# Passes of bias group 7 behind six rows of the last group, and later routing steps of the first sequence issued one by one

## The chip, the core and the metric

One core of a Trainium2 chip runs the whole kernel. Its engines run side by side, each in the order in which its instructions were issued: PE multiplies matrices, DVE and ACT work on rows, POOL issues most of the transfers, SP the others. They wait for each other by semaphores. The metric is the device time of the core in microseconds.

## The reference

Eight sequences of 576 positions go through attention with 8 heads of 64. The scores get a bias that a small network of 32 hidden units makes of the two positions alone. The result, 4608 tokens of 512, then goes through one of eight experts, named by the token's domain.

```python
scores = scale * np.matmul(q, k.transpose(0, 1, 3, 2))
x = (psi_rel / psi_i)[..., None]        # log1p(|i - j|) / log1p(max(i, 1))
bias = np.maximum(x @ w1 + b1, 0.0) @ w2
attn = softmax(scores + bias.transpose(2, 0, 1)[None])
x = (attn @ v).transpose(0, 2, 1, 3).reshape(4608, 512)
for e in range(8):
    mask = domain_id == e
    out[mask] = np.maximum(x[mask] @ w1[e], 0.0) @ w2[e]
```

## The kernel before

**Bias stage.** The bias depends on no input of a sequence, so it is made once. Nine groups (ib 0 to 8) of 64 query positions each take 16 rows: tiles hr of 128 x 576, four positions times 32 hidden units, made by DVE (L203) or ACT (L200). PE multiplies the rows with the output weights in three passes (L222, L227): key chunks 0 and 1, chunks 2 and 3, and the last 64 keys. Each pass fills one tile of a ring of three PSUM tiles (named sc). ACT takes the exponential of each pass (L237, L233, for the last group L244) into the bias tables biasM, biasR, biasL and biasRL. Of chunk 3 DVE also copies the raw bias of two heads (L241, into biasW), out of the tile of the second pass. The rows of group ib + 1 are issued ahead of the passes of group ib.

In between stand steps of other work: the routing steps (below), a memset of pad words (L254) with a DMA on SP that fills the buffer x_dram (L255, named fire_x, 9.25 MB), and the first transposes of q and k on PE, with the copies out of PSUM that at.take issues (L500, L509).

**Attention.** A round of units follows for each sequence. A unit (scores) is a pair of heads and a key chunk: m00 to m33 (head pair, chunk), r0 and r1 for the last 64 keys, l0, l1 and x for the last 64 queries. Each takes a tile of the same ring; PE writes scores into it, ACT takes the exponential (L562, named e) and DVE multiplies by the bias (L573), often two units at once. PE then multiplies by v (L586, L590, accumulator pu), and DVE divides by the sums (L616, L617). The order of units and other steps is written out by hand in ROUND. In the first sequence the last group's passes come behind units m03, m10 and m11, and the transposes of head pairs 2 and 3 behind unit m01.

**Routing.** A generator (_phase_route) yields after each of its small steps on DVE, which make of the domains the place posi of each token in x_dram. Each next(route) issues one step. Finished rows of a sequence are scattered by posi (L647).

**Experts.** x_dram is read back transposed (L792, tile xT) and each expert's two layers run on PE (L803, L779), with weights loaded by POOL (L741).

Of the kernel before, what the change touches and what calls it, by code (L numbers as in the profile page):

```python
# [68 lines left out]
def rap(t, off, dims, nparts=None):  # L69
    p0 = list(t.ap[0])  # L70
    if nparts is not None:
        p0[1] = nparts
    return bass.AP(tensor=t.tensor, offset=off, ap=[p0] + [list(d) for d in dims])
# [111 lines left out]
def _phase_bias(tc, G, route, at, x_dram):  # L185


    nc = tc.nc
    fsb = G.bias_pools.enter_context(tc.tile_pool(name="fsb", bufs=1, side="right"))
    def hidden(ib, between=None):  # L190
        hrl = []
        for k16 in range(16):
            if ib < 8:
                r, a = ib // 2, 16 * (ib % 2) + k16
                m, c0 = 32 * r + a, C4 - (16 * a + r)
            else:
                m, c0 = 128 + k16, W4 + C1 - 4 * k16
            hr = fsb.tile([P, S], F16, tag="hr", name="hr", bufs=34)
            if k16 in ((2, 5, 8, 11, 14) if ib < 2 else (3, 8, 13)):
                nc.scalar.activation(out=hr, in_=G.L4[:, c0: c0 + S], func=AF.Relu,  # L200
                                     bias=G.pb1[:], scale=G.slope[:, m: m + 1])
            else:
                nc.vector.tensor_scalar(out=hr, in0=G.L4[:, c0: c0 + S],  # L203
                                        scalar1=G.slope[:, m: m + 1], scalar2=G.nb1[:],
                                        op0=AO.mult, op1=AO.max)
            hrl.append(hr)
            if (ib, k16) == (0, 7):
                G.slopes(16, NGR)
            if (ib, k16) in ((1, 1), (1, 5), (1, 9), (2, 1), (2, 5)):
                next(route)  # L210
            if between is not None and k16 == between[0]:
                at.take(0, between[1])
        return hrl

    def outputs(ib, hrl):
        for jcs in ((0, 1), (2, 3), (4,)):
            eb = G.ring()
            for k16 in range(16):
                for lj, jc in enumerate(jcs):
                    hr = hrl[k16]  # L220
                    if jc < 4:
                        nc.tensor.matmul(out=eb[:, lj, 32 * k16: 32 * k16 + 32],  # L222
                                         lhsT=rap(hr, jc, [[4, 128]]),
                                         rhs=G.W2BIG[:, 0:32], start=True, stop=True)
                    else:
                        for h2 in range(2):
                            nc.tensor.matmul(out=eb[64 * h2: 64 * h2 + 64, 0, 16 * k16: 16 * k16 + 16],  # L227
                                             lhsT=hr[:, 512:576],
                                             rhs=rap(G.W2BIG, h2, [[2, 16]]), start=True, stop=True)
            ebv = eb.rearrange("p l (i h) -> p l h i", h=8)  # L230
            i0 = 64 * ib
            if jcs[0] == 4:
                nc.scalar.activation(out=G.biasR[:, :, i0: i0 + 64] if ib < 8 else G.biasRL,  # L233
                                     in_=eb[:, 0, 0:256].rearrange("p (i q) -> p q i", q=4),
                                     func=AF.Exp, bias=0.0, scale=0.125)
            elif ib < 8:
                nc.scalar.activation(out=G.biasM[:, jcs[0]: jcs[0] + 2, :, i0: i0 + 64], in_=ebv,  # L237
                                     func=AF.Exp, bias=0.0, scale=0.125)
                for lj, jc in enumerate(jcs):
                    if jc in RAW:  # L240
                        nc.vector.tensor_copy(out=G.biasW[jc][:, :, i0: i0 + 64], in_=ebv[:, lj, RAW[jc]:, :])  # L241
            else:
                for lj in range(2):
                    nc.scalar.activation(  # L244
                        out=G.biasL[:, jcs[0] // 2, lj, :, :, :].rearrange("p h q i -> p q h i"),
                        in_=ebv[:, lj, :, :].rearrange("p (q h) i -> p q h i", h=2),
                        func=AF.Exp, bias=0.0, scale=0.125)
            yield

    hrl = hidden(0)  # L250
    for ib in range(9):
        after = hidden(ib + 1, {6: (3, (4,)), 7: (1, (0, 1))}.get(ib)) if ib < 8 else None
        if ib == 1:
            nc.vector.memset(G.zero.rearrange("p o (r d) -> p (o r) d", r=4)[:, :, DM:].bitcast(I32), PAD)  # L254
            nc.sync.dma_start(out=x_dram.rearrange("(p c r) d -> p c (r d)", p=P, r=4),  # L255
                              in_=G.zero.to_broadcast([P, NSLOT // P // 4, 4 * XW]))
        for _ in outputs(ib, hrl):
            if ib == 8:
                yield
        if ib == 0:  # L260
            next(route)
        if ib in (5, 6):
            at.transposes(0, (4,) if ib == 5 else (0, 1), G.acc())
        if ib == 7:
            yield
        hrl = after


def _load_domains(tc, G, moe_domain_id):
# [140 lines left out]
class _Attention:  # L410
# [250 lines left out]
    def run(self, bias, route, late):  # L661
        G = self.G
        units = [("r", 0)] + [("m", p, c) for p in (0, 1) for c in range(4)] + [("r", 1)] + \
                [("m", 2, c) for c in range(4)] + [("l", 0), ("l", 1), ("x",)] + \
                [("m", 3, c) for c in range(4)]
        self.joined = {("l", 0): 0, ("l", 1): 1}
        for p in range(4):
            n = 4 if all(2 * p < RAW.get(c, H) for c in range(4)) else 2
            self.joined.update({("m", p, c): c % 2 for c in range(n)})
        names = {"".join(map(str, u)): ui for ui, u in enumerate(units)}  # L670
        jobs = {}

        def unit(b, name):
            if b >= B:
                return
            ui = names[name]
            jobs[b, name] = self.scores(b, units[ui])
            if b == 0 and name in LAST_ROWS:
                for _ in range(LAST_ROWS[name]):
                    next(bias, None)  # L680
            if (b, name) == (0, "m01"):
                self.transposes(0, (2, 3), G.acc())
                self.take(0, (2, 3))
            if b == 0 and ui > 2:
                for _ in range(2):
                    next(route, None)
            if b < B - 2 and ui == 3:
                self.load_qk(b + 2)
            if b < B - 2 and ui == 5:
                self.load_v(b + 2)  # L690
                self.load_last(b + 2)
            if b < B - 2 and ui == 7:
                self.load_vrag(b + 2)
            late(b, ui)

        def act(what, b):
            if what[0] in "TD":
                ps = tuple(map(int, what[1:]))
                if b + 1 < B:
                    if what[0] == "T":  # L700
                        self.transposes(b + 1, ps, self.G.ring())
                    else:
                        self.take(b + 1, ps)
            elif b < 0 or b >= B:
                pass
            elif what == "V":
                self.make_vext(b)
            elif what[0] == "W":
                self.weight(jobs.pop((b, what[1:])))
            elif what[0] == "A":  # L710
                p, c = int(what[1]), int(what[2])
                if c == 0:
                    self.av_begin(b, p)
                self.av(b, p, c)
                if (b, p) == (B - 1, 3) and c % 2 == 1:
                    self.norm(b, p, (c // 2,))
            elif what[0] == "N" and (b, int(what[1])) != (B - 1, 3):
                self.norm(b, int(what[1]))

        next(bias)  # L720
        unit(0, "r0")
        for b in range(B + 1):
            for what in ROUND:
                if what.rstrip("+") in names:
                    unit(b + what.count("+"), what.rstrip("+"))
                else:
                    act(what.rstrip("'"), b - what.count("'"))
# [162 lines left out]
def kernel(  # L890
# [24 lines left out]
    with tc.manual_schedule(engines={ET.PE, ET.DVE, ET.Activation}):  # L915
        with ExitStack() as att:
# [20 lines left out]
            at = _Attention(tc, G, q, k, v, x_dram)  # L937
            at.start()
            bias = _phase_bias(tc, G, route, at, x_dram)
            def late(b, ui):  # L940
                if (b, ui) == (0, 7):
# [47 lines left out]
```

## Time and profile before

| | us |
|---|---|
| median of three timed runs | 380.25 |
| lowest, highest | 378.14, 381.24 |
| profiled execution | 375.47 |
| its span, first to last instruction | 373.5 |
| busy: PE, DVE, ACT, POOL | 318.8, 234.9, 247.8, 181.4 |

The rows further down are from the profiled execution, with times from the start of its span. Its own time is 375.47 us, of which 373.5 are span. Bias rows and passes run until about 50 us, attention until about 216 us, the experts after that.

### The profile page before, as it was taken

Reading aid. Unit: us, or ns where it says so; the run is one execution under the profiler, and the core shown is the slowest. Engines: PE = TensorE matmul, PEld = TensorE weight load, DVE = VectorE, ACT = ScalarE, POOL = GpSimd, SP = SyncE. Lnnn points to the kernel's source line nnn. Section 1 sums busy time; section 2 is a strip of 40 time slices with the busy share of each in tenths; the row PEclk is TensorE's granted clock in tenths of the full one; section 3 lists DMA queues with packets and bytes.
Section 4 is the critical chain, followed back from the end, with each engine's and each line's share of the span. In section 5 each row is a group of like instructions: output and inputs, shape, how many; then the busy total and the mean of one; then the engine's idle time right before and its main releaser. Section 6 shows DMA issues by size and latency. Waiting matters only on the chain. (4 is left out here: it accounts for less than half of the span.)

```text
span 373.5 us, 9583 instructions
## 1 busy us (share of the span) xinstructions
PE 318.8 (85%) x4082; PEld 210.8 (56%) x4082; DVE 234.9 (63%) x436; ACT 247.8 (66%) x297; POOL 181.4 (49%) x220
## 2 busy tenths in 40 slices
PE   1499978689888888989897779999999699999892
PEld 0387946556565655656565545656463365565550
DVE  6999979899999999999999951221202002222121
ACT  8999969799999989999999933324150142332320
POOL 9360006318786888879664253525254027232322
PEclk9999999899999999999999999999999699999998
DMA  5999999989999999999998517999999999420212
GB/s 85 180 133 330 371 379 155 147 139 151 158 208 153 145 152 189 156 143 159 141 201 151 100 50 145 137 207 208 212 182 214 185 169 232 134 100 37 100 43 85
DMA packets 90995, 61.30 MB, mean 164 GB/s; under 512 B 43461, under 2 KB 85189, under 8 KB 90952
## 3 DMA queue, kind: packets, MB, share of 16 engines
q0 software_dynamic: 59904, 45.12, 74.6%
q1 hardware_dynamic: 31048, 15.57, 20.7%
q8 instruction: 32, 0.52, 0.5%
q14 instruction: 11, 0.09, 0.1%
HBM read 61.93 MB, written 24.70 MB: 232 GB/s over the span
## 5 line engine op out<-in xcount | busy, mean ns | idle before, releaser
L562 ACT ACTIVATE e<-sc 128x1024 f16<-128x1024 f32 x168 | 152.6, 1015 | 9.3 <-PE sc L534 5.6
L782 DVE COPY res<-ops 128x512 f32<-128x512 f32 x40 | 27.7, 692 | 117.8 <-PE ops L779 107.5
L841 ACT ACTIVATE hT<-hps 128x640 f16<-128x640 f32 x56 | 39.4, 704 | 86.5 <-PE hps L803 86.5
L573 DVE TENSOR_TENSOR e<-e,biasM 128x2048 f16<-128x2048 f16 x64 | 72.9, 1150 | 0.2
L779 PE MATMUL ops<-w,hT 128*128 128x512 f16 x320 | 70.5, 379 | 0.0
L803 PE MATMUL hps<-xT,w 128*128 128x320 f16 x448 | 64.8, 307 | 5.3 <-DMA xT<-fire_x 4.2
L783 POOL DMA_INDIRECT out_dram<-res,ids x40 | 39.9, 997 | 50.7 <-DVE res L782 37.9
L534 PE MATMUL sc<-qkT 64*128 64x512 f16 x256 | 45.7, 389 | 16.1 <-ACT e L562 13.3
L803 PEld LDWEIGHTS <-w 128*128 128x128 f16 x448 | 44.8, 100 | 25.6 <-issue 5.0
L741 POOL DMA_DIRECT2D w<-in_moe_w_dram x32 | 27.9, 890 | 49.8 <-DMA w<-in_moe_w_dram 21.1
L779 PEld LDWEIGHTS <-hT 128*128 128x128 f16 x320 | 31.2, 98 | 36.5 <-ACT hT L815 0.3
L647 POOL DMA_INDIRECT fire_x<-xt,posi x32 | 45.8, 1433 | 11.0 <-issue 8.8
L590 PE MATMUL pu<-vext,e 128*128 128x65 f16 x1024 | 47.5, 196 | 4.0 <-DVE e L573 4.0
L590 PEld LDWEIGHTS <-e 128*128 128x128 f16 x1024 | 43.1, 99 | 6.6 <-DVE e L573 4.9
L203 DVE TENSOR_SCALAR hr<-L,slope,nb 128x576 f16<-128x576 f16 x113 | 40.9, 428 | 0.0
L222 PE MATMUL sc<-W2BIG,hr 128*128 128x32 f16 x576 | 26.7, 193 | 12.3 <-DVE hr L203 9.7
L534 PEld LDWEIGHTS <-qkT 64*128 64x128 f16 x256 | 12.3, 94 | 36.6 <-issue 30.2
L222 PEld LDWEIGHTS <-hr 128*128 128x128 f16 x576 | 22.4, 116 | 17.0 <-DVE hr L203 12.9
L586 PE MATMUL pu<-vrag,e 128*128 128x130 f16 x128 | 28.6, 223 | 2.1 <-DVE xl L633 1.4
L647 POOL DMA_INDIRECT fire_x<-xl,posi x8 | 10.3, 1286 | 34.9 <-DVE e L573 15.1
L200 ACT ACTIVATE hr<-L,pb,slope 128x576 f16<-128x576 f16 x31 | 24.5, 859 | 0.8 <-DVE slope L166 0.8
L617 DVE TENSOR_TENSOR xt<-pu,rz 128x512 f16<-128x512 f32 (+1 forms) x33 | 22.3, 675 | 1.5
(129 smaller groups left out, 356.6 us busy)
## 6 DMA issues: line engine op xcount, KB each, us to landing
w<-in_moe_w_dram POOLq DMA_DIRECT2D x32, 512.0 KB, 7.6
fire_x<-zero SPq DMA_DIRECT2D x1, 9252.0 KB
qn<-in_q_dram POOLq DMA_DIRECT2D x8, 512.0 KB, 6.2
kn<-in_k_dram POOLq DMA_DIRECT2D x8, 512.0 KB, 9.5
vst<-in_v_dram POOLq DMA_DIRECT2D x8, 512.0 KB, 7.1
out_dram<-res,ids POOLq DMA_INDIRECT x40, 8.7
last<-zero SPq DMA_DIRECT2D x2, 256.0 KB, 3.0
last<-in_q_dram POOLq DMA_DIRECT2D x16, 32.0 KB, 9.0
```

Of the source, the lines that this page charges most:

```text
L203: nc.vector.tensor_scalar(out=hr, in0=G.L4[:, c0: c0 + S], scalar1=G.slope[:, m: m + 1], scalar2=G.nb1[:], op0=AO.mult, op1=AO.max)
L222: nc.tensor.matmul(out=eb[:, lj, 32 * k16: 32 * k16 + 32], lhsT=rap(hr, jc, [[4, 128]]), rhs=G.W2BIG[:, 0:32], start=True, stop=True)
L534: mm(out=sc[:, h2, :], lhsT=self.qkT[b, p][hs[h2], 1, 128 * c: 128 * c + 128], rhs=self.qkT[b, p][hs[h2], 0, :], start=not raw, stop=True)
L562: nc.scalar.activation(out=ef[:, 0:n], in_=sf[:, 0:n], func=AF.Exp, bias=0.0, scale=0.125)
L573: self.nc.vector.tensor_tensor(out=job[0], in0=job[0], in1=job[1], op=AO.mult)
L586: mm(out=self.pu[:, c // 2, o: o + 130], lhsT=er[:, p % 2, 128 * c: 128 * c + 128], rhs=vr[:, p, :], start=True, stop=False, skip_group_ch ...
L590: mm(out=self.pu[:, c // 2, o + 65 * h2: o + 65 * h2 + 65], lhsT=self.e[b, ("m", p, j)][:, h2, 128 * c: 128 * c + 128], rhs=vx[:, 2 * p + ...
L647: inst = self.nc.gpsimd.indirect_dma_start(out=self.x_dram[:, :], out_offset=bass.IndirectOffsetOnAxis(ap=self.G.posi[0:n, c:c + 1], axis= ...
L779: nc.tensor.matmul(out=ops_, lhsT=hT[:, fc, t0: t0 + 128], rhs=G.w.w2(e, fc), start=(fc == 0), stop=(fc == 7))
L783: inst = nc.gpsimd.indirect_dma_start(out=out[:], out_offset=bass.IndirectOffsetOnAxis(ap=idx.bitcast(I32), axis=0), in_=res[:], in_offset ...
L803: nc.tensor.matmul(out=hps[:, i, 0:HC], lhsT=G.w.w1(e, dc, fc), rhs=xT[:, dc, HC * hf: HC * hf + HC], start=(dc == 0), stop=(dc == 3))
L841: nc.scalar.activation(out=hT[:, fc, :].rearrange("p (a b) -> p a b", a=2), in_=first(e, xT, ((fc, 0), (fc, 1))), func=AF.Relu, bias=0.0, ...
```

## The change

The generator of the rows now yields after each row, so that passes may be issued between rows. The passes of group 7 are issued behind the first six rows of group 8 instead of behind all sixteen; for the other groups it stays at all sixteen. The three rows of group 8 that ACT makes are k16 2, 3 and 4 instead of 3, 8 and 13. The memset of pad words and the fill of x_dram are issued ahead of the rows of group 2, not behind them. In the first sequence one routing step instead of two follows each unit from the eleventh unit on.

```diff
-    def hidden(ib, between=None):
-        hrl = []
+    def rows(ib, hrl):
         for k16 in range(16):
...
-            if k16 in ((2, 5, 8, 11, 14) if ib < 2 else (3, 8, 13)):
+            if k16 in ((2, 5, 8, 11, 14) if ib < 2 else (3, 8, 13) if ib < 8 else (2, 3, 4)):
...
-            if between is not None and k16 == between[0]:
-                at.take(0, between[1])
-        return hrl
+            if (ib, k16) in ((7, 3), (8, 1)):
+                at.take(0, (4,) if ib == 7 else (0, 1))
+            yield
...
     for ib in range(9):
-        after = hidden(ib + 1, {6: (3, (4,)), 7: (1, (0, 1))}.get(ib)) if ib < 8 else None
+        later = []
+        ahead = rows(ib + 1, later) if ib < 8 else iter(())
         if ib == 1:
...
-        for _ in outputs(ib, hrl):
+        for _ in range(6 if ib == 7 else 16):
+            next(ahead, None)
+        for _ in outputs(ib, now):
             if ib == 8:
                 yield
+        for _ in ahead:
+            pass
...
             if b == 0 and ui > 2:
-                for _ in range(2):
+                for _ in range(2 if ui < 10 else 1):
                     next(route, None)
```

The order of PE, ACT, POOL and SP's instructions stays the same. On DVE three places change. The line numbers of the changed kernel are other ones: its L202, L240, L515, L579 are L203, L241, L509, L573 before.

On DVE, from the last rows of group 7 to the first bias product, before (qkT is what take issues, first for head pairs 0 and 1, then for 2 and 3):

```order
L203 TENSOR_SCALAR hr<-L_110,slope,nb_120 128x576 x10
L241 CAST biasW_73<-sc 128x2x64
L203 TENSOR_SCALAR hr<-L_110,slope,nb_120 128x576 x2
L509 COPY qkT<-pu 128x2048
L203 TENSOR_SCALAR hr<-L_110,slope,nb_120 128x576 x11
L241 CAST biasW_73<-sc 128x2x64
L509 COPY qkT<-pu 128x2048
L573 TENSOR_TENSOR e<-e,biasR 128x1024
```

The same place on DVE in the changed kernel:

```order
L202 TENSOR_SCALAR hr<-L_110,slope,nb_120 128x576 x10
L240 CAST biasW_73<-sc 128x2x64
L202 TENSOR_SCALAR hr<-L_110,slope,nb_120 128x576 x2
L515 COPY qkT<-pu 128x2048
L202 TENSOR_SCALAR hr<-L_110,slope,nb_120 128x576
L240 CAST biasW_73<-sc 128x2x64
L202 TENSOR_SCALAR hr<-L_110,slope,nb_120 128x576 x10
L515 COPY qkT<-pu 128x2048
```

The copy of raw bias of group 7 has moved ahead of ten rows of group 8.

On DVE, from the routing steps behind the first division of the first round on, before (e_1604 is the pair of units m12 and m13, e with biasR is r1, e_1677 is m20 and m21):

```order
L376 TENSOR_TENSOR incl<-incl,past 128x320
L378 TENSOR_TENSOR incl<-incl,oh 128x320
L381 TENSOR_REDUCE posf<-incl 128x40
L573 TENSOR_TENSOR e_1604<-e_1604,biasM 128x2048
L573 TENSOR_TENSOR e<-e,biasR 128x1024
L383 SCALAR_TENSOR_TENSOR posf<-domf,posf 128x40
L387 CAST posi<-posf 128x40
L573 TENSOR_TENSOR e_1677<-e_1677,biasM 128x2048
```

The same place on DVE in the changed kernel:

```order
L382 TENSOR_TENSOR incl<-incl,past 128x320
L579 TENSOR_TENSOR e_1604<-e_1604,biasM 128x2048
L579 TENSOR_TENSOR e<-e,biasR 128x1024
L384 TENSOR_TENSOR incl<-incl,oh 128x320
L387 TENSOR_REDUCE posf<-incl 128x40
L389 SCALAR_TENSOR_TENSOR posf<-domf,posf 128x40
L393 CAST posi<-posf 128x40
L579 TENSOR_TENSOR e_1677<-e_1677,biasM 128x2048
```

Two routing steps have moved behind two bias products.

On DVE, at the rows of group 2 (the thirteen rows, with the copy L329 between), before:

```order
L321 CAST rowtot_369<-incl 128x16
L203 TENSOR_SCALAR hr<-L_110,slope,nb_120 128x576 x5
L329 COPY apref<-pu 128x32
L203 TENSOR_SCALAR hr<-L_110,slope,nb_120 128x576 x8
L254 MEMSET zero 128x4
L241 CAST biasW_73<-sc 128x2x64
```

The same place on DVE in the changed kernel:

```order
L327 CAST rowtot_369<-incl 128x16
L256 MEMSET zero 128x4
L202 TENSOR_SCALAR hr<-L_110,slope,nb_120 128x576 x5
L335 COPY apref<-pu 128x32
L202 TENSOR_SCALAR hr<-L_110,slope,nb_120 128x576 x8
L240 CAST biasW_73<-sc 128x2x64
```

The memset, for which the fill of x_dram on SP waits, has moved ahead of the thirteen rows.

## Rows read from the trace of the kernel before

**Rows 1.** Windows, 75 to 216 us: length, busy by engine, granted clock, DMA, GB/s
```profile
75.00:216.00 141.00, 121.91 (x2078) 84.81 (x2077) 135.68 (x195) 136.67 (x152) 96.08 (x107) 1.00 1.05 155
```

**Rows 2.** Waits of DVE, 75 to 204 us: total, times, longest
```profile
DVE rz L616 <- PE pu L590: 1.1, 6, 0.2
```

**Rows 3.** Waits of ACT, 75 to 215 us
```profile
ACT e L562 <- PE sc L534: 2.6, 5, 0.5
```

**Rows 4.** Timeline of DVE, 46 to 58 us: start, duration, work [idle before, releaser]
```profile
49.14 3.82 DVE L203 TENSOR_SCALAR hr<-L,slope,nb 128x576 f16<-128x576 f16 x11
52.89 0.27 DVE L241 CAST biasW<-sc 128x128 f16<-128x128 f32 x1
55.71 1.22 DVE L509 COPY qkT<-pu 128x2048 f16<-128x2048 f16 x1 [2.55 <-PE pu L475]
```

**Rows 5.** Timeline of DVE, 65 to 76 us
```profile
67.72 0.49 DVE L378 TENSOR_TENSOR incl<-incl,oh 128x320 f32<-128x320 f32 x1
...
68.93 1.22 DVE L573 TENSOR_TENSOR e<-e,biasM 128x2048 f16<-128x2048 f16 x1
...
70.99 1.22 DVE L573 TENSOR_TENSOR e<-e,biasM 128x2048 f16<-128x2048 f16 x1
73.25 0.21 DVE L616 RECIPROCAL rz<-pu 128x8 f32<-128x8 f32 x1 [1.04 <-PE pu L590]
```

**Rows 6.** Timeline of PE, 49 to 62 us
```profile
50.54 0.61 PE L534 MATMUL sc<-qkT 64*128 64x512 f16 x2
53.21 0.61 PE L534 MATMUL sc<-qkT 64*128 64x512 f16 x2 [2.06 <-DVE biasW L241]
...
55.03 0.64 PE L475 MATMUL pu<-idn,kn 128*64 128x128 f16 x8
...
61.12 0.41 PE L475 MATMUL sc<-idn,qn 128*64 128x128 f16 x8 [0.30 <-ACT biasL L244]
```

**Rows 7.** Timeline of ACT, 44 to 78 us
```profile
47.72 2.04 ACT L237 ACTIVATE biasM<-sc 128x1024 f16<-128x1024 f32 x2 [0.75 <-PE sc L222]
...
53.86 1.02 ACT L562 ACTIVATE e<-sc 128x1024 f16<-128x1024 f32 x1 [1.27 <-PE sc L534]
56.25 1.94 ACT L562 ACTIVATE e<-sc 128x1024 f16<-128x1024 f32 x2 [1.37 <-PE sc L534]
...
62.57 4.69 ACT L562 ACTIVATE e<-sc 128x1024 f16<-128x1024 f32 x5 [0.30 <-PE sc L534]
...
72.16 1.02 ACT L562 ACTIVATE e<-sc 128x1024 f16<-128x1024 f32 x1 [1.30 <-PE sc L547]
73.86 5.13 ACT L562 ACTIVATE e<-sc 128x1024 f16<-128x1024 f32 x6 [0.69 <-PE sc L547]
```

**Rows 8.** Timeline of PE, 66 to 76 us
```profile
70.20 0.51 PE L590 MATMUL pu<-vext,e 128*128 128x65 f16 x6 [2.28 <-DVE e L573]
```

**Rows 9.** Windows of PE, 70 to 74 us: length, busy, granted clock, DMA, GB/s
```profile
70.00:74.00 4.00, 3.80 (x59) 0.57 0.96 135
```

**Rows 10.** Timeline of PE, 213 to 222 us
```profile
217.06 0.23 PE L586 MATMUL pu<-vrag,e 128*128 128x130 f16 x1 [1.41 <-DVE xl L633]
217.12 0.42 PE L590 MATMUL pu<-vext,e 128*128 128x65 f16 x8
```

**Rows 11.** Timeline of SP, 20 to 30 us
```profile
23.42 0.60 SPq L255 DMA_DIRECT2D fire_x<-zero  x1
```

**Rows 12.** DMA issues, 22 to 23 us: size, us from issue to landing
```profile
vst<-in_v_dram POOLq DMA_DIRECT2D x1, 512.0 KB, 19.1
```

**Rows 13.** Timeline of POOL, 0 to 130 us
```profile
21.00 1.18 POOL L445 DMA_DIRECT2D kn<-in_k_dram  x1 [2.76 <-DMA vst<-in_v_dram]
```

**Rows 14.** Windows of PE, 56 to 58 us, columns as in rows 9
```profile
56.00:58.00 2.00, 2.00 (x38) 1.00 0.61 117
```

**Rows 15.** Timeline of PE, 228 to 374 us
```profile
271.22 8.85 PE L803 MATMUL hps<-xT,w 128*128 128x320 f16 x64
...
292.95 11.66 PE L803 MATMUL hps<-xT,w 128*128 128x320 f16 x64 [4.24 <-DMA xT<-fire_x]
```

More of the change, by code (lines that the diff above doesn't have):

```diff
@@ L248, in outputs @@
             yield
-    hrl = hidden(0)
+    now = []
+    for _ in rows(0, now):
+        pass
     for ib in range(9):
-        after = hidden(ib + 1, {6: (3, (4,)), 7: (1, (0, 1))}.get(ib)) if ib < 8 else None
+        later = []
+        ahead = rows(ib + 1, later) if ib < 8 else iter(())
         if ib == 1:
@@ L256, in _phase_bias @@
                               in_=G.zero.to_broadcast([P, NSLOT // P // 4, 4 * XW]))
-        for _ in outputs(ib, hrl):
+        for _ in range(6 if ib == 7 else 16):
+            next(ahead, None)
+        for _ in outputs(ib, now):
             if ib == 8:
                 yield
+        for _ in ahead:
+            pass
         if ib == 0:
@@ L265, in _phase_bias @@
             yield
-        hrl = after
+        now = later
 def _load_domains(tc, G, moe_domain_id):
```

## The prediction

> **What bounds the kernel now.** I read the slices of the page first. Three stages show: the bias stage to about 50 us, the attention rounds to about 216 us, then the expert layers, in which PE alone is nearly always busy. The change touches the bias stage's last group and the first attention round, so the question is what that shortens and whether the rest of the run passes it on.
>
> The windows view settles the middle: from 75 to 216 us DVE is busy 135.68 and ACT 136.67 of 141 us [rows 1], PE 121.91. Both are full, and the waits tell which is the tighter one: in those rounds DVE waits for PE 1.1 us in six small pieces [rows 2], ACT 2.6 us in five for one kind of matmul alone [rows 3]. So DVE's chain sets the pace, ACT a little behind, and a microsecond in which DVE stood still before 75 us is worth a microsecond at the end of attention. The expert layers start from the last scatter of attention, so they move with it unless something in them keeps its own time (the last rival).
>
> Where does DVE stand still before 75 us? In two places. At 53.16 it has finished the copy of raw bias (L241) and sits 2.55 us until PE's transposes of head pairs 2 and 3 are there [rows 4]. At 72.2 it sits 1.04 us until PE has finished an accumulation [rows 5]. The change stands at both.
>
> **Part 1: the passes of group 7.** PE may not start the score unit m01 before the ring tile of group 7's second pass is free, and that tile's last reader is DVE's copy L241. In order on DVE stand: two rows of group 8, the copy of head pairs 0 and 1, eleven more rows (49.14 to 52.96), then L241 at 52.89 [rows 4]. PE has m00 done at 51.15 and waits 2.06 us for it; m01 starts at 53.21 [rows 6]. The four blocks of transposes behind m01 are what DVE's 2.55 us wait is for, and ACT shows the same hole twice, 1.27 and 1.37 us [rows 7].
>
> Now one row instead of eleven stands ahead of L241. When can it run? DVE reaches it at 49.14 plus one row; eleven rows take 52.89 less 49.14 = 3.75 us, so one is 0.34: 49.48. But L241 waits for ACT too, which evicts the same tile: its two evictions end at 47.72 + 2.04 = 49.76 [rows 7]. So DVE waits 0.28 us there (a new wait; ten rows of group 8 queue behind it) and is done at 49.76 + 0.27 = 50.03. That is before PE finishes m00, so m01 follows m00 at once: PE's 2.06 us go.
>
> What is late next? DVE has ten rows from 50.03, at 0.34 each: 53.4 us. PE's transposes, done at 55.03 + 0.64 = 55.67 before [rows 6], end 2.06 earlier at 53.6. The copy behind them starts at 53.6 instead of 55.71. The two chains nearly tie: DVE's ten rows have 0.2 us to spare, and a later copy would cost beyond that. ACT's exponential of m01 can start at most 1.27 us earlier, when ACT is free; the one of m02 starts 2.06 earlier, so ACT's holes shrink from 2.64 to about 0.6 us together. PE needs the rows of group 8 only behind the transposes, m02 and m03, so after 53.6, when the last of them are done. **Gain 2.06 us**; bounds 1.8 (the tie goes 0.3 the wrong way) to 2.2 (55.71 less 53.5).
>
> Three rows of group 8 go to ACT as before, other ones and the same number, in the same place ahead of the evictions: nothing.
>
> **Part 2: two routing steps.** From unit 10 on one routing step instead of two follows each unit of the first sequence, and on DVE this changes one place: the product of incl with oh and the reduction to posf (67.72 to 68.93, so 1.21 us) [rows 5] now stand behind the bias product of units m12 and m13 and that of r1, instead of ahead of them. Both products' inputs are ready by then: ACT's run of five exponentials that holds m12, m13 and r1 ended at 62.57 + 4.69 = 67.26 [rows 7], and these are its first three. PE stands 2.28 us for the first of them, until 70.20 [rows 8]. So PE resumes 1.21 us earlier and its wait is 1.07.
>
> On DVE the same work is done in another order, so the product at 70.99 starts when it did. Behind it stands the 1.04 us wait for PE [rows 5]; with PE 1.21 earlier the accumulator is ready at 73.25 less 1.21 = 72.0, before DVE arrives at 72.2. **Gain on DVE 1.04 us.** The position table is finished at the same place in DVE's order, so the scatters of the first sequence see no difference. ACT's two holes here, 1.30 and 0.69 us [rows 7], also wait for PE. They shrink by 1.21 if PE keeps its pace, and by all 1.99 if it gets faster.
>
> [...] Behind a wait of 1.41 us late in attention eight matmuls of the same kind take 0.42 [rows 10], where six take 0.51 at 70.20. [...]
>
> But the next 141 us are DVE's more than ACT's, so the sum takes DVE's 1.04. Bounds: nothing (the accumulator comes late for another reason) and 1.99.
>
> **Part 3: the fill of the scatter buffer.** The memset of the pad words, and the 9.25 MB fill of x_dram that waits for it, came behind 13 rows of group 2 and go out now before them: 13 rows of 0.34 us make 4.4, so the fill goes out at 19.0 instead of 23.42 [rows 11]. It meets the loads of the second sequence, and the first of them that PE needs are q and k, for the transposes at 61.12 [rows 6], now 59. Rows of this trace bound the cost. v of that sequence, which is issued behind k and so nearly all in competition with the fill, landed after 19.1 us [rows 12]; if k, issued at 21.0 [rows 13], takes as long, it is there at 40. At worst k stands still while the fill runs. The fill ended within 56 to 58, where the rate falls to 117 GB/s [rows 14], some 33 us after its issue; now that is 52, and the 512 KB of k at 117 GB/s take 4.5 us: 56.5, still in time. So nothing, from either end.
> [...]
>
> **Sum**: 2.06 + 1.04 = 3.10 us. The profiled execution took 375.47 (373.5 of it span), so it would be 372.4. The median of the three timed runs is 380.25, 4.8 above it, and they spread over 3.1 us; I take the same difference off the median: **377.15**, which is 0.8% less. A change under 1% can hardly be told from none with this kernel.
>
> **Rivals.**
> First: only the first wait pays. Something other than the moved steps holds the accumulator at 72 us, or the DVE rows end later than 53.6. For it speaks the near tie of part 1 and that the second gain is small; against it that every input of the moved product is on record as ready. Gain some 2.06: 378.2.
>
> Second: ACT's chain sets the end after all. It would be so if PE stays at full clock through 70 to 74 us and DVE's own rounds get shorter by its little waits. For it: ACT is busy 1 us more than DVE in 75 to 216. Against: ACT's waits there are over twice DVE's. Gain 2.06 + 1.99 = 4.05: 376.2.
>
> Third: the change does not do what it says, because L241 is held by ACT as well. It decides if ACT's second eviction ends near 52.9 instead of 49.76; nothing in ACT's order changes ahead of it. 380.25.
>
> Fourth, the other side: the expert layers give more back than attention gains. At 292.95 PE has waited 4.24 us for the transposed rows of expert 4, and the layer then takes 11.66 us where the same layer of an earlier expert takes 8.85 [rows 15]. That transfer shares the DMA engines with the weights. [...] Against it: the fetches wait for PE and for the last scatter, which move. For it: it is the one stall of the expert layers, and the timed runs, 2.7 to 5.8 us over the profiled one, show that something differs from run to run.
>
> **How the numbers follow.** Forecast 0.55, first rival 0.16, second 0.16, third 0.06, fourth 0.07. Half the spread of the timed runs is 1.55, so from the second rival's 376.2 down to 374.6, and from the first's 378.2 up past 379.8 to the third's 380.3: 374.6 to 380.3. One per cent is 3.8 us, so faster means below 376.45. The forecast lies 0.7 above that, less than half the spread, and gives about a third of its chance (0.19); the second rival over half (0.1); the first some 0.03: 0.33 with a little rounding. Slower by over 1% needs the fourth: 0.06. The rest, 0.61, is no change.
>
> **What would show it.** PE's 2.06 us wait on L241 gone, m01 right behind m00, and L241 at about 49.8. DVE's wait before the copy at 55.71 down from 2.55 to 0.3 or less. PE's wait of 2.28 down to about 1.1 and DVE's 1.04 gone; the granted clock in the matching 4 us above 0.57 or not. The fill issued near 19 us, with no wait of PE for qn or kn. The last scatter of attention some 3.1 us earlier, and the wait for xT of expert 4 near 4.2. Wrong would be: a new wait of DVE in the rounds, a PE wait for rows of group 8, or a much longer wait for xT.

## The result, and the profile after

| | before | after |
|---|---|---|
| median of 22 executions each, us | 380.19 | 382.88 |
| lowest, highest | 374.75, 394.71 | 370.28, 400.41 |
| ratio of the comparable executions | | 0.9869 (0.9824 to 0.9915) |
| profiled execution, its span | 375.47, 373.5 | 372.06, 370.1 |

Executions of either kernel spread over 20 us and more, so the ratio is taken between those within 1.5% of the fastest of their kernel, and the plain medians, which go the other way, are not used. In a second measurement (12 executions against 17) the ratio was 0.9912 (0.9855 to 0.9969), and there the plain medians, 369.57 against 375.48, go the same way. The prediction, 377.15 of 380.25, is a ratio of 0.9918; held against the plain median of the changed kernel, 382.88, it would be 5.7 us too low.

In the profiled execution the chain of DVE in the bias stage now reads as follows; it answers to [rows 4] (start, duration, instruction, idle time ahead of it and what ended it).

```profile
46.61 0.29 DVE L240 CAST biasW<-sc 128x128 f16<-128x128 f32 x1
...
48.62 0.43 DVE L202 TENSOR_SCALAR hr<-L,slope,nb 128x576 f16<-128x576 f16 x1
50.23 0.29 DVE L240 CAST biasW<-sc 128x128 f16<-128x128 f32 x1 [1.18 <-ACT biasM L236]
50.44 3.50 DVE L202 TENSOR_SCALAR hr<-L,slope,nb 128x576 f16<-128x576 f16 x10
53.92 1.22 DVE L515 COPY qkT<-pu 128x2048 f16<-128x2048 f16 x1
```

The copy of raw bias (L241 before, L240 now) stands behind one row, and the copy of head pairs 2 and 3 starts at 53.92 without a wait; before it waited 2.55 us and started at 55.71. The new wait ahead of the raw copy is 1.18 us where the prediction had 0.28. The timeline of PE in the same stretch, for [rows 6], and that of ACT, for [rows 7], show why:

```profile
45.57 0.83 PE L221 MATMUL sc<-W2BIG,hr 128*128 128x32 f16 x20
47.58 1.56 PE L221 MATMUL sc<-W2BIG,hr 128*128 128x32 f16 x44 [1.18 <-DVE hr L202]
...
51.00 1.04 PE L540 MATMUL sc<-qkT 64*128 64x512 f16 x4
...
53.24 0.64 PE L481 MATMUL pu<-idn,kn 128*64 128x128 f16 x8
```

```profile
48.16 2.04 ACT L236 ACTIVATE biasM<-sc 128x1024 f16<-128x1024 f32 x2 [1.42 <-PE sc L221]
...
51.10 2.86 ACT L568 ACTIVATE e<-sc 128x1024 f16<-128x1024 f32 x3 [0.58 <-PE sc L546]
54.31 1.94 ACT L568 ACTIVATE e<-sc 128x1024 f16<-128x1024 f32 x2 [0.36 <-PE sc L540]
```

m00 and m01 run without a gap (four products from 51.00), so PE's 2.06 us wait for the raw copy is gone. Of ACT's holes the one of 1.27 us is gone (its exponentials run on from 51.10) and the one of 1.37 is 0.36; the 0.58 stood at this place before too, as 0.57. But PE paused 1.18 us inside the passes of group 7, 0.35 before. The releaser named, DVE's rows, can't be it: the last row of group 7 was written at 46.6 (the raw copy of group 6 follows it at 46.61). More on this pause below.

At the second place, PE first and then DVE (for [rows 5, 8]), and the granted clock of the stretch behind (for [rows 9]; the last three columns are the clock, the DMA share and GB/s):

```profile
66.96 0.37 PE L596 MATMUL pu<-vext,e 128*128 128x65 f16 x6 [0.98 <-DVE e L579]
```

```profile
69.08 1.22 DVE L579 TENSOR_TENSOR e<-e,biasM 128x2048 f16<-128x2048 f16 x1
70.22 0.20 DVE L622 RECIPROCAL rz<-pu 128x8 f32<-128x8 f32 x1
```

```profile
75.00:216.00 141.00, 120.11 (x2028) 83.32 (x2027) 131.65 (x188) 133.75 (x149) 94.58 (x107) 1.00 1.04 150
67.00:71.00 4.00, 3.43 (x69) 2.95 (x69) 3.86 (x8) 4.00 (x7) 2.38 (x3) 1.00 1.16 179
```

PE's wait went from 2.28 to 0.98 us, DVE's 1.04 is gone, and the clock of the stretch behind it is 1.00 instead of 0.57. DVE copies v for the second round (L478 now, L472 before) at 78.46; in the kernel before it did so at 81.49. So a lead of 3.0 us was there (before, then after):

```profile
81.49 0.69 DVE L472 COPY vext<-vst 128x2048 f16<-128x2048 f16 x1
```

```profile
78.46 0.69 DVE L478 COPY vext<-vst 128x2048 f16<-128x2048 f16 x1
```

It did not reach the end of attention in this execution: the first row of the window view above, which answers to [rows 1], has DVE at 131.65 of 141 us where it was 135.68. The expert layers' first product started at 220.10, later than the 219.22 of before. Two new waits of DVE took it, of which the first reads so on DVE, and so on PE:

```profile
86.70 0.21 DVE L622 RECIPROCAL rz<-pu 128x8 f32<-128x8 f32 x1 [2.06 <-PE sc L481]
```

```profile
86.05 0.26 PE L481 MATMUL sc<-idn,kn 128*64 128x128 f16 x2
86.68 0.34 PE L481 MATMUL sc<-idn,kn 128*64 128x128 f16 x5 [0.37 <-issue]
87.41 0.22 PE L481 MATMUL sc<-idn,kn 128*64 128x128 f16 x1 [0.38 <-issue]
```

PE stops twice inside a row of eight transposes whose inputs are in one tile, waiting for nothing that the profile shows; a second such place at 186 us cost DVE 1.76. What the profiled execution won in the end, 3.4 us, it won in the expert layers, where the 4.24 us wait for expert 4 was not there (answering to [rows 15]):

```profile
290.20 8.86 PE L809 MATMUL hps<-xT,w 128*128 128x320 f16 x64
```

So it was luck that this execution, at 372.06 us, came out beside the 372.4 of the forecast: two of its steps, attention handing the lead on and the experts keeping their time, failed in it in opposite directions. The experiments had to tell what of that belongs to the change.

### The profile page after: what moved, and what is told of

It is laid out like the page before. It is cut to its first block, busy times and chain, and to the rows that moved or that the text cites. A ratio compares the mean times of both kernels' runs of the same rounds, so it can differ in the third digit from the quotient of the medians.

```text
span 370.1 us, 9584 instructions
## 1 busy us (share of the span) xinstructions
PE 315.5 (85%) x4082; PEld 208.6 (56%) x4082; DVE 234.3 (63%) x436; ACT 246.8 (67%) x297; POOL 179.2 (48%) x220
## 5 line engine op out<-in xcount | busy, mean ns | idle before, releaser
L579 DVE TENSOR_TENSOR e<-e,biasM 128x2048 f16<-128x2048 f16 x64 | 73.0, 1150 | 0.1
L785 PE MATMUL ops<-w,hT 128*128 128x512 f16 x320 | 70.5, 379 | 0.0
L809 PE MATMUL hps<-xT,w 128*128 128x320 f16 x448 | 62.4, 299 | 2.8 <-ACT hT L847 1.8
L809 PEld LDWEIGHTS <-w 128*128 128x128 f16 x448 | 43.7, 98 | 21.6 <-issue 2.2
L653 POOL DMA_INDIRECT fire_x<-xt,posi x32 | 43.6, 1363 | 11.0 <-issue 9.4
L202 DVE TENSOR_SCALAR hr<-L,slope,nb 128x576 f16<-128x576 f16 x113 | 40.6, 431 | 0.0
L221 PE MATMUL sc<-W2BIG,hr 128*128 128x32 f16 x576 | 25.5, 192 | 13.3 <-DVE hr L202 11.5
```

The lines of the kernel that those rows point to most:

```text
L202: nc.vector.tensor_scalar(out=hr, in0=G.L4[:, c0: c0 + S], scalar1=G.slope[:, m: m + 1], scalar2=G.nb1[:], op0=AO.mult, op1=AO.max)
L221: nc.tensor.matmul(out=eb[:, lj, 32 * k16: 32 * k16 + 32], lhsT=rap(hr, jc, [[4, 128]]), rhs=G.W2BIG[:, 0:32], start=True, stop=True)
L579: self.nc.vector.tensor_tensor(out=job[0], in0=job[0], in1=job[1], op=AO.mult)
L653: inst = self.nc.gpsimd.indirect_dma_start(out=self.x_dram[:, :], out_offset=bass.IndirectOffsetOnAxis(ap=self.G.posi[0:n, c:c + 1], axis= ...
L785: nc.tensor.matmul(out=ops_, lhsT=hT[:, fc, t0: t0 + 128], rhs=G.w.w2(e, fc), start=(fc == 0), stop=(fc == 7))
L809: nc.tensor.matmul(out=hps[:, i, 0:HC], lhsT=G.w.w1(e, dc, fc), rhs=xT[:, dc, HC * hf: HC * hf + HC], start=(dc == 0), stop=(dc == 3))
```

## The experiments

The table gathers, from the trace of each run, where DVE copies v for the second round, where the first expert product starts, and what lies between and behind. Behind the dots the rows are the changed kernel or a variant of it.

| run | v copy | experts start | between | from there to the end of the span |
|---|---|---|---|---|
| before | 81.49 | 219.22 | 137.73 | 154.3 |
| e8, before again | 82.25 | 220.02 | 137.77 | 169.3 |
| e5, before, cut | 82.29 | 219.66 | 137.37 | |
| e3, fill alone | 81.17 | 218.47 | 137.30 | 174.4 |
| e1, rows alone | 80.16 | 217.84 | 137.68 | 155.3 |
| e2, routing alone | 80.89 | 218.67 | 137.78 | 148.3 |
| ... | | | | |
| after | 78.46 | 220.10 | 141.64 | 150.0 |
| e7, after again | 78.49 | 216.24 | 137.75 | 154.3 |
| e12, after again | 78.20 | 215.54 | 137.34 | 152.4 |
| e6, after, cut | 79.50 | 217.27 | 137.77 | |
| e9, no late weights | 78.57 | 215.91 | 137.34 | 145.2 |
| e10, ten rows ahead | 79.18 | 216.96 | 137.78 | 148.1 |
| e4, fill late | 77.93 | 215.36 | 137.43 | 155.1 |
| e11, fill late again | 78.10 | 215.91 | 137.81 | 147.0 |

The times between are 137.3 to 137.8 us in thirteen of fourteen executions. A lead at the second round comes out whole at the end of attention; the first profiled execution of the changed kernel is the exception. The first expert products of before and of e7:

```profile
219.22 7.07 PE L813 MATMUL hps<-xA,w 128*128 128x512 f16 x32
```

```profile
216.24 7.07 PE L819 MATMUL hps<-xA,w 128*128 128x512 f16 x32
```

**e1, the rows alone.** The changed kernel with the other two edits undone:

```diff
-                for _ in range(2 if ui < 10 else 1):
+                for _ in range(2):
```

and the memset and fill back behind the rows of group 2.

> The kernel before with the first part alone: six rows of group 8 ahead of the passes of group 7 (and its three ScalarE rows moved as in the change); fill and routing steps as before. My theory (each part pays by its own wait, and DVE passes it on): DVE's 2.55 us wait before the second copy of transposes goes, the 2.28 and 1.04 us waits of the routing stay, DVE starts the second round (its product behind the copy of v) 1.8 to 2.1 us earlier than at 82.09, the kernel is 0.5% shorter: 0.995 of the kernel before, some 378. Rival A (ScalarE's chain or PE's instruction supply takes it back in the bias stage): under 1 us earlier there, ratio 0.998 to 1. Rival B (the gain over the kernel before comes from the fill that goes out earlier, not from the waits): second round earlier, but the end of attention and the total as before, 1.000.

```profile
49.81 0.29 DVE L240 CAST biasW<-sc 128x128 f16<-128x128 f32 x1 [0.24 <-ACT biasM L236]
53.49 1.23 DVE L515 COPY qkT<-pu 128x2048 f16<-128x2048 f16 x1
60.85 1.23 DVE L515 COPY qkT<-sc 128x2048 f16<-128x2048 f16 x1 [1.02 <-PE sc L481]
71.86 0.21 DVE L622 RECIPROCAL rz<-pu 128x8 f32<-128x8 f32 x1 [1.05 <-PE pu L596]
```

The copy starts at 53.49 instead of 55.71, 2.22 us earlier from the same start (47.14 and 47.12 for the raw copy of group 6), and the raw copy stands at 49.81 behind 0.24 us: the places of the prediction nearly to the tenth. At the second round 1.33 is left, less than the 1.8 to 2.1 expected, since the transposes of the second sequence ran at a lower clock here (0.57 granted in 58 to 62 us; eight took 0.64 to 0.68 us, in before 0.41 or 0.42) and DVE waited 1.02 us for them, where it waited 0.18 in the profile of before. Executions of the kernel before with the same 1.02 (e5, e8) copy v at 82.29 and 82.25, and against those it is 2.1. The timed ratio, 0.9971 (0.9899 to 1.0043), can't tell 0.995 from 1.

**e2, the routing alone.** The kernel before with the one line of the routing steps, `2 if ui < 10 else 1`.

> The kernel before with the second part alone: one routing step instead of two from unit 10 on. My theory: PE's 2.28 us wait goes to about 1.1 us and DVE's 1.04 us wait goes, the granted clock of the stretch behind stays full, DVE starts the second round 1.0 to 1.2 us earlier than at 82.09, ratio 0.997 (379). Rival A (the two parts hang together: the accumulator is late for another reason until the first part is in): no difference at the second round, 1.000. Rival B (ScalarE sets the end): 2 us, 0.995.

The 1.04 us wait of DVE is gone. From its copy near 62 us to the copy of v it took 18.1 us; with the old routing it is 19.2 to 19.7 in five executions, 19.39 in the mean, and with the new one 18.1 to 18.4 in nine, mean 18.20. That is 1.19 us for the second part, whether the first is in or not, so rival A falls. The second round starts at 80.89: only 0.60 before the 81.49 of before, less than expected, but 1.4 before the executions that had the same wait for transposes (1.01 here). The timed ratio, 1.0008 (0.9961 to 1.0055), contains the 0.997.

**e3, the fill alone, and e4 and e11, everything but the fill.** e3 is the kernel before with the memset and the fill moved ahead of the rows of group 2; e4 and e11 are the changed kernel with them moved back:

```diff
-        if ib == 1:
-            nc.vector.memset(G.zero..., PAD)
-            nc.sync.dma_start(out=x_dram..., in_=G.zero...)
         for _ in range(6 if ib == 7 else 16):
             next(ahead, None)
+        if ib == 1:
+            nc.vector.memset(G.zero..., PAD)
+            nc.sync.dma_start(out=x_dram..., in_=G.zero...)
```

> The kernel before with the third change alone: memset and fill of the scatter buffer ahead of the rows of group 2. My theory: the fill is issued some 4.4 to 5.3 us earlier, near 18 us, nothing on the path sees it, second round at 82 us, ratio 1.000 within the uncertainty. Rival A (the earlier fill moves all later transfers and so is what shortened the expert layers): ratio 0.99, with no wait of PE for the transposed rows of expert 4. Rival B (the earlier fill holds up the loads of the first two sequences): a PE or POOL wait for qn, kn or vst, the second round later than 82.1, ratio above 1.003.

> The changed kernel with the fill of the scatter buffer put back behind the rows of group 2; rows of group 8 and routing steps as changed. My theory: the second round starts near 79.1 as in the changed kernel, ratio to the kernel before the same as that of the change, 0.987 to 0.992. Rival (the fill carries part of the gain or of the spread between executions): ratio 0.992 to 1.000, or a spread of the timed executions that differs clearly from the 370 to 400 us of the changed kernel.

> The changed kernel with the fill put back behind the rows of group 2 once more, beside the changed kernel on the same chip. My theory (the fill's place costs and brings nothing): the same time as the changed kernel, within 0.5% between comparable executions, and a spread of the same size. Rival (the earlier fill disturbs the executions): 0.5% or more below the changed kernel, and a spread half as wide.

In e3 the fill is issued at 18.30 instead of 23.42 [rows 11] and the second round starts at 81.17; ratio 1.004 (0.9969 to 1.0111). No PE wait for q, k or v shows. Nor does it carry the gain of the expert layers: e3 has the longest of all, 174.4 us. e4 and e11 keep the whole of the change at the second round (77.93, 78.10) with ratios of 0.9931 (0.9876 to 0.9985) and 0.9833 (0.9755 to 0.991); beside e11 the changed kernel itself had 0.9912. By time both missed what was expected: the ratio of e4 lies just inside its rival's range and its executions spread by 8.1 us only, and e11 is 0.75% below the changed kernel, as its rival had it, though with a spread of 25 us against 21. The two ratios differ from that of the change in opposite directions, and the intervals overlap.

But the fill is not free. PE paused after the twentieth product of group 7 in twelve of the fourteen executions of the table. With the fill late the pauses are 0, 0, 0.17, 0.21, 0.23, 0.33 and 0.35 us; with the fill early 0.23, 0.53, 0.76, 0.88, 1.15, 1.18 and 1.49. After the twentieth product of group 6 it paused 0.20 to 1.34 us in four of the seven with the fill early (e3, after, e6, e9) and in none of the seven with it late. The kernel before covers the pause in group 7: from the raw copy of group 6 to the copy of head pairs 2 and 3 it takes 8.59 to 8.61 us in five executions, the 1.49 of e3 among them. With six rows ahead it is 6.32, 6.35 and 6.67 with the fill late, and 6.54 to 8.17 (mean 7.15 of five) with it early. So, counted from that raw copy, the early fill costs 0.7 us of what the rows gain. By the time of the span it is less: the copy of head pairs 2 and 3 starts at 53.71 in the mean of the five and at 53.50 in that of the three, because in the five the raw copy of group 6 came 0.5 earlier. The cost is 0.2 to 0.7 us. The 0.75% between the comparable executions of e11 (364.8 in the mean) and e12 (367.6), 2.8 us, is more than that, and the rest of it would lie in the expert layers (147.0 against 152.4 in the profiles); twelve executions do not settle whether the fill's place matters there.

**e5 and e6, both kernels without experts 1 to 7.**

```diff
-    for e in range(E):
+    for e in range(1):
```

and no fetch of their rows.

> The kernel before with experts 1 to 7 left out (their layers and the loads and writes that belong to them; the rows of the output that they would write stay unwritten), so that what is timed is the bias stage, attention and one expert layer. My theory is that the differences of 10 to 20 us between executions come from the expert layers, whose weights and transposed rows arrive at a different time in each; then these executions spread by less than 5 us, at some 238 us (375.5 less seven layers of some 19.6). Rival: the spread comes from attention (PE's instruction supply, the clock) and stays at 10 us or more.

> The changed kernel with experts 1 to 7 left out in the same way. My theory (the change gains its 3.1 us ahead of the second round and DVE carries them to the end of attention): 2.5 to 3.3 us less than the kernel before cut in the same way. [...] Rival B (only the first wait pays): 1.3 to 2.1 us less.

The spread fell to 3.4 us (253.44 to 256.87) and 2.4 (253.13 to 255.57), from 26 us for the whole kernel in the same session (370.4 to 396.21): nearly all of it comes from the expert layers, whose length in the table differs by 27 us in the whole kernels with all their loads, where the start of the experts differs by 4.7. The level, 255, is above my 238: behind the one layer the span goes on until five late loads of weights and the writes are done. Medians are 255.48 and 253.90, 1.58 apart, so here the time missed what I expected and fell where rival B had it. Rival B's mechanism is not in the trace, though: both waits are gone. In e6 PE came to the passes of group 7 later than anywhere else (46.51, elsewhere 45.1 to 46.0) and paused 1.15, DVE waited 2.05 us for the raw copy, and the experts start 2.39 us before those of e5; 0.6 of that is given back behind. Whether the unprofiled executions lost the rest in the same way is open.

**e7, e8 and e12, both kernels again.**

> The changed kernel once more, for its profile. My theory (the two waits of some 2 us behind PE's transposes near 86 and 186 us belong to that one execution, not to the change): none of them, the second round at 78 to 79 us, the last product of attention 3 us earlier than 219.2, 216 us. Rival (they belong to the order of the change, which puts PE's fetch of instructions at a bad place): the same two waits at the same two places.

> The kernel before once more, for its profile. My theory (the 4.24 us wait for the transposed rows of expert 4 differs from execution to execution): the second round at 81 to 82 us and the expert layers starting within 1 us of 219.2, but other waits for transposed rows or weights, at other experts, or none. Rival (that wait belongs to the order of the work): 3.5 to 5 us at expert 4 again.

> The changed kernel itself, timed beside the two variants. My theory: 0.987 to 0.993 of the kernel before among comparable executions, the second round at 78 to 79.5 us, the expert layers starting near 216.3 us unless PE stands for instructions. Rival (the expert layers give it back): 1.000.

The waits of PE in the expert layers of e7 (timeline) and of e8 (waits from 216 us on: total, times, longest):

```profile
272.32 10.53 PE L809 MATMUL hps<-xT,w 128*128 128x320 f16 x64 [3.57 <-DMA xT<-fire_x]
292.75 8.85 PE L809 MATMUL hps<-xT,w 128*128 128x320 f16 x64 [1.27 <-DMA xT<-fire_x]
```

```profile
PE hps L803 <- DMA xT<-fire_x: 9.3, 2, 6.3
PE ops L779 <- DVE res L782: 7.4, 2, 6.0
```

Neither wait of 2 us near 86 and 186 is in e7 or e12, or in any other of the fourteen executions: they belonged to that one. The wait for transposed rows stood at expert 4 in before; in e7 it stood at expert 3 and, smaller, at 4, in e12 at 3 alone, in e8 it was 9.3 us at 3 and 5, in after, e2, e10 and e11 there was none. So it goes with the execution, not with the order of the work or the change. The second round of e8, 82.25, was just later than expected; e12 started its second round at 78.20, as expected, and its experts at 215.54, 0.8 earlier.

**e9, no weights loaded in the expert layers.** The changed kernel, experts 4 to 7 on the weights of 0 to 3:

```diff
-            G.w.load(1, G.w_late)
+            pass
...
-        return _block(self.t[e, dc // 2], dc, fc)
+        return _block(self.t[e % 4, dc // 2], dc, fc)
```

and the same in w2.

> The changed kernel without the loads of weights inside the expert layers (experts 4 to 7 are computed with the weights of experts 0 to 3, so the same number of products on other numbers). My theory (the spread between executions comes from the weights' transfers, which share the DMA engines with the transposed rows): no wait of PE for transposed rows or weights over 0.5 us, the expert layers take some 148 us from the first of their products to the end of the span, and the executions spread by less than 5 us, near 366. Rival (the transposed rows are late by themselves, or behind the writes of results): waits of 2 to 6 us for the transposed rows of some expert stay, and a spread of 10 us or more.

All that PE waited for in its expert layers:

```profile
PE hps L809 <- DVEq L837: 0.9, 1, 0.9
```

No wait for rows or weights, 145.2 us of expert layers, and executions from 363.06 to 366.23 where the changed kernel beside it had 365.43 to 386.79. Without these loads the rows come in time and six executions lie within 3.2 us (8.1 in e4, which had the loads). So the late rows and the spread need the loads, and the rival falls. How the loads do it is not shown: without them their traffic on the DMA engines is gone (in the window from 216 to 395 us the mean share of the engines is 0.31; in e11, with the loads, 0.68), but so are their issues on POOL (busy 43.13 us there against 56.75). That loads and transposed rows move at one time shows in before: from 288 to 293 us the packets of the queue that has POOL's transfers took 93.2% of the 16 engines' time, those of SP's queue, with the transposed rows, 36.8%. Nor is it weights and transposed rows alone: in the two longest profiles, e3 and e8, PE waited another 8.7 and 7.4 us for DVE's copies of results (the second line of e8 above), and the longest such copy in e8 had waited 7.68 us for a write of results:

```profile
320.32 0.69 DVE L782 COPY res<-ops 128x512 f32<-128x512 f32 x1 [7.68 <-DMA out_dram<-res,ids]
```

**e10, ten rows ahead instead of six** (`range(10 if ib == 7 else 16)`).

> The changed kernel with ten rows of group 8 ahead of the passes of group 7 instead of six, so that DVE runs five more rows instead of one before the copy of raw bias. My theory (DVE's rows and PE's transposes tie, so what DVE waits for ScalarE before that copy is lost only in name): the wait of 0.2 to 2.1 us before the copy of raw bias is gone, a wait for PE's transposes of up to as much stands before the copy of head pairs 2 and 3 instead, the second round starts at 78 to 79.5 us as with six rows, and the time is that of the changed kernel within 0.5%. Rival A (the wait before the raw copy is lost time, which the rows can cover): 0.5 to 1.2 us earlier at the second round, below 78. Rival B (PE waits for the raw copy again, as in the kernel before): 0.5 us or more later, 79.5 or above.

DVE, then PE:

```profile
50.79 0.34 DVE L240 CAST biasW<-sc 128x128 f16<-128x128 f32 x1
53.68 1.22 DVE L515 COPY qkT<-pu 128x2048 f16<-128x2048 f16 x1 [0.51 <-PE pu L481]
```

```profile
50.44 1.35 PE L540 MATMUL sc<-qkT 64*128 64x512 f16 x4
```

The wait moved, as expected, from the raw copy to the copy of transposes. The copy comes 6.60 us after the raw copy of group 6, against 6.32 of e11, which had the same pause of 0.23 us: PE's four products took 1.35 instead of 1.04 because the raw copy now came 0.3 late for m01. So rows and transposes do tie, and more rows ahead cover nothing here. With a pause of a microsecond it was not tried. e4 shows the tie from the other side: PE had no pause there and took 0.39 us for eight transposes (0.64 in after), so they were done at 51.3, 2 us earlier than in e11, and still the copy started at 53.56, when DVE's ten rows were done (PE, then DVE):

```profile
50.91 0.39 PE L481 MATMUL pu<-idn,kn 128*64 128x128 f16 x8
```

```profile
49.59 4.05 DVE L202 TENSOR_SCALAR hr<-L,slope,nb 128x576 f16<-128x576 f16 x10
53.56 1.21 DVE L515 COPY qkT<-pu 128x2048 f16<-128x2048 f16 x1
```

The timed ratio of e10, 0.9865 (0.9723 to 1.0006), tells nothing more.

## Why the prediction held, point by point

**Part 1, 2.06 us.** The mechanism was right: the raw copy no longer holds m01, the second copy starts without a wait, and the tie of rows and transposes is there (e10, e4). The wait before the raw copy, 0.28 in the sum, was mis-sized: it is 0 to 2.05 us, by PE's pause in group 7. With the fill late the part measures 8.60 less 6.45, the mean of three, 2.15 us; as the change stands, with the fill early, 8.60 less 7.15, 1.45 us, which is below the forecast's lower bound of 1.8.

**Part 2, 1.04 us.** Measured 1.19 over fourteen executions; PE's wait 0.98 in after where 1.07 was forecast, 0.67 to 1.25 in the nine with the new routing. Whether PE would get faster behind the shorter wait was the open step. In seven of the nine the granted clock stayed full (1.00 in after); in e12 and e9, behind 1.14 and 1.25 us, it fell all the same, and [rows 10], with the clock at 1.00 behind 1.41 us (217 to 218 us), was no safe guide (e12, 0.57, granted clock third from the end):

```profile
67.00:71.00 4.00, 4.00 (x61) 3.97 (x58) 3.86 (x9) 3.30 (x4) 2.39 (x3) 0.57 1.08 146
```

DVE's wait is gone in these two as well (18.3 and 18.4 us from copy to copy), so the gain did not hang on the clock. In the order before, behind a wait of 2.06 to 2.50 us, the clock fell in all five executions (in before 0.50 from 70.5 to 73 us, 0.57 over the four of [rows 9]). What brings it down is not shown. The second rival's 1.99 us for ACT did not come, whether the clock stayed up (after) or fell (e12): in after ACT's holes of 1.30 and 0.69 are gone, but one of 1.15 stands behind its next seven exponentials, and in e12 two of 0.70 and 0.30 are left, so ACT won 0.8 to 1.0 us.

```profile
74.01 6.64 ACT L568 ACTIVATE e<-sc 128x1024 f16<-128x1024 f32 x7 [1.15 <-PE sc L540]
```

**Part 3, nothing.** This is the term that was wrong. I had sought what the earlier fill would do to the loads that PE waits for, and there it did nothing (it went out at 18.14, not 19.0, and still moved packets in 54 to 56 us, not 52). But with it goes a longer pause of PE, and part 1 has just taken away the rows that covered it: 0.2 to 0.7 us.

**The sum.** Experts start at 219.63 in the mean of three executions of the order before (before, e5, e8) and at 216.24 in four of the change (e6, e7, e9, e12): 3.4 us, against 3.10. The execution with PE's two stops (after) is left out; with it the lead would be 2.6. The terms for the four: 1.49 (8.60 less 7.11, the mean of the four) and 1.18, 0.30 because the raw copy of group 6 came earlier (46.55 against 46.85), and 0.35 because eight transposes near 60 us took 0.64 to 0.69 us instead of 0.41 or 0.42 in two of the three (e5, e8) and in one of the four (e7), at 0.84 us each. The last two are of the executions, not shown to be of the change. So the change's own share is 2.7 us, with part 1 half a microsecond short, and that the lead came out within 0.3 us of 3.10 is in part luck. DVE handed the lead on whole, 137.3 to 137.8 us between: the step from [rows 1 to 3] held.

**The first and third rival** fall with e1 and e2: each wait goes by itself and moves the second round. (The time of e6 against e5, 1.58 us, would suit the first, and is not fully explained.) **The fourth** asked whether the expert layers keep their own time. They do not eat the lead; they vary by more than it, 147 to 174 us, and in the profiled pair happened to make up for 3.9 us that PE's stops had cost. That they lose over 1% to the change, the 0.06 of the forecast, no run shows. The measured ratio, 0.9869, is 1.9 us better than forecast, and its interval ends just short of 0.9918; it makes 5.0 us, 1.6 more than the lead, and nothing here shows where they come from. The second measurement, 0.9912, lies on the forecast, and its 3.3 us agree with the lead. I gave 0.61 to a difference within 1%: the first measurement is just outside, the second inside.

## What to carry to other kernels

Where a wait is taken away by moving cover, look for what else that cover hid: eleven rows hid a pause of PE that no row of the profile named rightly. To size a change of under 1% in a kernel whose end is noisy, compare the start times of the stage behind the change over several profiles, not the totals: here the experts started within 0.8 us of each other in three executions of the order before and within 1.7 us in four of the change, while totals moved by 20. And a difference between two single profiles belongs to the change only if it comes again.

## What the hardware did that I had not expected

PE's pause in group 7 comes after the same product in each execution. In the DMA view a packet of 0.02 MB on the queue named instruction (q8) falls shortly ahead; in slices of a quarter microsecond it is at 45.00 in the changed kernel:

```profile
q8 instruction: 1, 0.02, 22.0%
```

In the twelve executions with a pause PE goes on 2.4 to 2.6 us after the start of that slice (after: 47.58; before: 44.50 and 47.13; e3: 45.50 and 48.11). In the two without (e4, e5) the packet is at 44.00 and 43.75, so the same 2.5 us end about when PE gets there. The profile names DVE's rows as the releaser, in e9 and e12 the raw copy, for the same pause:

```profile
47.01 1.56 PE L221 MATMUL sc<-W2BIG,hr 128*128 128x32 f16 x44 [0.76 <-DVE biasW L240]
```

I read it as PE waiting for its instructions; no trace shows what it waits for. In PE's order, weight loads counted, the twentieth products of groups 6 and 7 are 256 instructions apart, and PE of the changed kernel paused at both (0.62 and 1.18 us). It takes a small product with its load of weights every 40 ns here (0.83 us for twenty) and pauses up to 1.49 us. That the early fill goes with the longer pauses is seen in fourteen executions; that it does so by making the packet late, and how, was not tried. The stops near 86 and 186 us do not fit it: the packets of that queue around them start near 79.7, 91.9, 176.3 and 186.7 us, none of them some 2.5 us ahead of 86.68 or 186.39, where PE went on after its first stop. Their cause is open.

The other surprise was the clock near 60 us: eight transposes took 0.62 to 0.69 us in seven executions and 0.41 or 0.42 in the seven others, of both kernels, which moved DVE by up to 0.84 us (a wait of 1.02 instead of 0.18). The windows view of e1 and that of after, both 58 to 62 us, granted clock third from the end:

```profile
58.00:62.00 4.00, 3.69 (x73) 2.60 (x73) 2.92 (x6) 2.64 (x5) 1.57 (x3) 0.57 1.68 148
```

```profile
58.00:62.00 4.00, 3.33 (x88) 2.60 (x88) 3.80 (x10) 3.69 (x7) 3.78 (x8) 1.00 1.35 173
```
